# Two ABAB layers on one Trainium2 core: another layout of q and k in the attention, another order of its first steps

## The chip, the cores and the metric

The program runs on one core of one Trainium2 chip. The metric is the device time of one execution in microseconds (us); lower is better. A kernel is run several times and its median is given. Beside it there is one execution taken by the hardware profiler, whose rows are quoted here.

The engines are TensorE (PE in the profile, with its weight loads as PEld), VectorE (DVE), ScalarE (ACT), GpSimd (POOL) and SyncE (SP). PSUM is the small memory into which TensorE writes its sums, in banks of 512 float32 per partition; SBUF holds everything else, with 128 partitions.

## The reference

The program applies A, B, A, B to x (2048 tokens, 576 features), each with a layer norm ahead of it and a residual behind it; both A use the same weights, and so do both B. A is attention with 32 heads of 18 features. A token looks at itself and at the seven tokens at distances 2, 4, ..., 14 before it:

```
W, dil = (8, 2)
qkv = (x @ wqkv).reshape(B, S, 3, H, Dh)            # H = 32, Dh = 18
off = jnp.arange(W) * dil
idx = pos[:, None] - off[None, :]
mask = idx >= 0
...
logits = jnp.einsum('bhsd,bhswd->bhsw', q, kg) * Dh ** (-0.5)
logits = jnp.where(mask[None, None, :, :], logits, -1000000000.0)
o = jnp.einsum('bhsw,bhswd->bhsd', softmax(logits), vg) @ wo
```

B is a gated layer: gelu of x @ w_in (576 to 4608), a layer norm on its second half, a product over tokens with the 2048 x 2048 matrix w_sp, the product with the first half, and w_out back to 576 features.

## The kernel before

Activations are held in bfloat16, features on partitions (xnT) for matmuls that contract over features. The four layers follow each other in program order; there is no barrier between them, and each engine works through its own queue in order.

**The attention layer** (`layer_A`, once as the first layer, li = 0, once as the third, li = 2). Queries and keys of all heads stand in one SBUF tile QK of [128, 2, 8, 2048]: partitions, q or k, group, token. A head h lies in group g = h // 4, in the 32-partition slot j = h % 4: 18 partitions of data, then 14 "window rows", which hold a pattern that makes the logits of tokens outside the window so small that their exponential vanishes. The matmul over the 32 rows of a slot thus gives the masked logits of one head.

The window rows are written by VectorE (`fill_window_rows`, L198 and L201): four copies over all 128 partitions for each half of the tokens, each over one of q and k and four groups. They write over the data rows too, so the data come after them: half 0 of the data comes after `fill_window_rows(QK, 0)`, half 1 after `fill_window_rows(QK, 1)`.

The data come by way of a stage. A projection unit PG (L442; its matmuls are on L422) computes, for a chunk d of 128 features of q or of k (d = 0 to 3; d = 4 holds the last 64 features of q and of k) and a 512-token column cc, five matmuls into a PSUM bank; `evac` casts it into a stage tile (L403 on VectorE, L405 on ScalarE). When the four units of one chunk and one 1024-token half are there, one DMA per head and chunk ("move", issued through the helper on L78) carries the head's rows from the stage to its slot in QK, with two runs of 2 KB per partition (q and k). A head whose features straddle two chunks needs two moves. The moves go out alternately on two queues, GpSimd's and SyncE's; d = 4 needs a move each for q and k. SyncE also issues the transposes of the normalised input (L265).

Attention steps: the queries are cut into NT = 17 tiles (120 query columns each, 128 keys), each tile in two halves of 16 heads (groups 0 to 3, then 4 to 7), so NST = 34 steps s = 2t + half. Step loop: logits of the next step (`L_mm`, L496: 16 matmuls of 32 x 128), their exponential on ScalarE (`EXP`, L505), then the product with v of the present step (`PV`, L519, into a bank O_ps), which VectorE divides by the sums (reciprocal L525, product L527); then what a table has put at that step: the remaining projection units (cast by VectorE), the units VW that compute v, the output projection WO, loads, copies of the transposed output (`O_CP`).

PSUM in the steps: L_ps has four banks; all else (O_ps, pp, pv, pw) goes round through three banks, the ring "PT". A matmul into a bank waits until its last reader is done.

Before the steps: in the first attention the ten (chunk, column) pairs of half 0 are projected by PG units cast on ScalarE; then follow six units "pre" of the second half, whose casts k_ = 0 to 3 go to VectorE. After two of them comes `L_mm(0)`, after the fourth `fill_window_rows(QK, 1)`. In the third layer `PG_run` (L425) computes the units of d = 0, 1 and then 2, 3 with their banks all open, `on_dve` naming the units that VectorE casts; then `fill_window_rows(QK, 1)`, the two units of d = 4, four tiles of v, `L_mm(0)`, the six pre units and the steps.

In the first attention the layer norm of x runs just ahead, tile by tile: statistics S_ (L673), power on GpSimd (R_, L686: GpSimd does `R_(12, 4)` between moves), scaling A_ (L693), transpose T_ by DMA.

**Layer B** (L946, L1070, L1094, L1143) is dense matmuls. At its end each 128-token tile gets its residual, is stored, and is normalised for the next attention: statistics and power, with the scaling on ScalarE.

Of the kernel before, what the change touches and what calls it, by code (L numbers as in the profile page):

```python
# [18 lines left out]
P = 128  # L19
# [44 lines left out]
class K:  # L64
# [129 lines left out]
    def fill_window_rows(self, QK, half):  # L194
        nc, n = self.nc, self.cfg.S // 2
        for g0 in (0, 4):
            for a in range(2):
                nc.vector.tensor_copy(out=QK[:, a, g0:g0 + 4, half * n:(half + 1) * n].rearrange("p g (k x) -> p g k x", x=P),  # L198
                                      in_=self.pat[:, a, half, None, None, :].to_broadcast([P, 4, n // P, P]))
            if half == 0:  # L200
                nc.vector.tensor_copy(out=QK[:, :, g0:g0 + 4, 0:8], in_=self.pat0[:, :, None, :].to_broadcast([P, 2, 4, 8]))  # L201

# [137 lines left out]
    def layer_A(self, li):  # L340
# [11 lines left out]
        QK = main.tile([P, 2, 8, XW], bf16, name="QK")  # L352
        qT, kT = QK[:, 0], QK[:, 1]
        NSTG, CBW = (3 if li == 0 else 4), 1024
        stgs = [main.tile([P, 2, CBW], bf16, name=f"stg{k_}") for k_ in range(NSTG if li == 0 else 2)]
# [86 lines left out]
        def PG(d, qk, cc, dve, queues=(nc.sync, nc.gpsimd), pp=None):  # L442
# [18 lines left out]
            evac(stg[:, qk, gi * 512:(gi + 1) * 512], pp, dve)  # L461
            stg_left[key] -= 1
            if stg_left[key] == 0:
                stg_tiles.pop(key)
                cs = slice(cc * 512, (cc + 1) * 512) if alone else slice(cb * CBW, (cb + 1) * CBW)
                ss = slice(gi * 512, (gi + 1) * 512) if alone else slice(0, CBW)
                moves = []
                for h in range(d * P // DH, H):
# [14 lines left out]
        NST = 2 * NT  # L483
        L_tiles = {}
        owed = []

        def L_mm(s):
            t, hf = divmod(s, 2)
            nk, nq = tdim(t)
# [3 lines left out]
            for ftl in range(4):  # L493
                g = 4 * hf + ftl
                for j in range(4):
                    nc.tensor.matmul(L_tiles[s][j // 3][:nk, j % 3, ftl * P:ftl * P + nq],  # L496
                                     lhsT=kT[32 * j:32 * j + 32, g, k0_(t):k0_(t) + nk],
                                     rhs=qT[32 * j:32 * j + 32, g, q0_(t):q0_(t) + nq],
                                     start=True, stop=True, tile_position=(32 * j, 0))

        def EXP(s):
            nk, nq = tdim(s // 2)
            for jp, L_ps in enumerate(L_tiles.pop(s)):
                Lv = L_ps[:].rearrange("p a (b c) -> p a b c", c=P)
                nc.scalar.activation(out=P_bufs[2 * jp + s % 2][:nk, :, :, 0:nq], in_=Lv[:nk, :, :, 0:nq], func=ACT.Exp,  # L505
# [5 lines left out]
        def PV(s):  # L511
# [3 lines left out]
            for jp, js in enumerate(((0, 1, 2), (3,))):  # L515
                for ftl in range(4):
                    for jj, j in enumerate(js):
                        idx = 4 * ftl + j
                        nc.tensor.matmul(O_ps[:, idx * (DH + 1):(idx + 1) * (DH + 1)],  # L519
                                         lhsT=P_bufs[2 * jp + s % 2][:nk, jj, ftl, :],  # L520
# [24 lines left out]
        def O_CP(t):  # L545
# [710 lines left out]
```

## Time and profile before

| | us |
|---|---|
| median of 3 runs | 1163.04 (1162.76 to 1164.21) |
| profiled execution | 1164.2 |
| its span | 1162.4 |
| TensorE busy | 1146.0 |
| VectorE busy | 559.4 |
| ScalarE busy | 339.0 |
| GpSimd busy | 271.0 |

The profile's rows are read so. A row of a timeline has the start (us from the start of the span), the length, the engine, the line, the operation, the tiles written and read, the shape, the count of instructions that are drawn together, and in brackets the idle time before and what ended it. A row of waits has the engine and line that waited, what it waited for, the us in total, how often, and the longest. A row of windows has a stretch and the busy time of each engine in it, then the clock granted to TensorE (1.00 is full), the share of the DMA engines and GB/s. A row of the chain of waits has start, length, and who held the chain. "x11: 502/587/4973" is count and minimum, median and maximum in ns.

### The profile page before, as it was taken

How to read it: one execution, taken by the hardware profiler on the slowest of the kernel's cores; microseconds unless marked ns; L12 is line 12 of the kernel's file. 1: busy time of each engine (PE TensorE's matmuls, PEld its weight loads, DVE VectorE, ACT ScalarE, POOL GpSimd, SP SyncE). 2: the span in 40 equal slices, each digit the busy share in tenths (PEclk: the TensorE clock that was granted, in tenths of full speed). 3: DMA queues.
4: the chain of work that ended last, by engine and by line, in shares of the span. 5: the costliest groups of instructions: out<-in, count | busy, mean ns of one | idle time of the engine just before them, and what ended most of it. 6: DMA issues, size and time to landing. Idle time of an engine off the chain costs nothing.

```text
span 1162.4 us, 19969 instructions
## 1 busy us (share of the span) xinstructions
PE 1146.0 (99%) x8163; PEld 610.5 (53%) x8258; DVE 559.4 (48%) x1183; ACT 339.0 (29%) x503; POOL 271.0 (23%) x375
## 2 busy tenths in 40 slices
PE   9899999999999999999999999999999999999998
PEld 5467544444444444457755774444444444444677
DVE  8679888322233222235475888862322223322321
ACT  5499455011110111102247884541011110011000
POOL 3769855000000000001163776540000000000000
PEclk9899999999999999999999999999999999999999
DMA  9599796000000000049656997920000000001332
GB/s 214 114 177 291 199 219 132 23 12 12 12 2 11 12 12 1 19 138 297 172 102 117 229 245 183 259 55 4 8 12 12 12 12 1 12 1 47 114 104 74
DMA packets 184600, 106.59 MB, mean 92 GB/s; under 512 B 136201, under 2 KB 165545, under 8 KB 184509
## 3 DMA queue, kind: packets, MB, share of 16 engines
q1 hardware_dynamic: 171821, 86.04, 32.4%
q0 software_dynamic: 6096, 13.38, 4.4%
q10 hardware_dynamic: 6592, 5.90, 1.7%
q8 instruction: 64, 1.05, 0.4%
q14 instruction: 27, 0.22, 0.1%
HBM read 42.54 MB, written 21.77 MB: 55 GB/s over the span
## 4 chain that ended last, share of the span: by engine, by line
PE 94%; issue 1%; POOL 1%; ACT 1%; DVE 1%; DMA 1%; SPq 0%; ACTq 0%; DVEq 0%; POOLq 0%
PE pg L1094 43%; PE po L1143 12%; PE pz L946 6%; PE pz L1070 6%; PE pz1s L1070 6%; PE pzs L946 6%; PE pp L422 5%; PE pw L587 3%; PE O_ps L519 3%; PE pv L411 3%; PE L_ps L496 2%; POOL QK L78 1%; ACT P_sb L505 1%; DMA x_in<-in_A_x_dram 0%; DVE QK L198 0%
## 5 line engine op out<-in xcount | busy, mean ns | idle before, releaser
L1094 PE MATMUL pg<-Wq,Z 128*128 128x512 bf16 x2260 | 497.9, 379 | 2.5
L1094 PEld LDWEIGHTS <-Z 128*128 128x128 bf16 x2304 | 225.4, 98 | 271.8
L1098 DVE TENSOR_TENSOR g_tmp<-pg,ln_xn 128x512 f32<-128x512 f32 x144 | 99.6, 692 | 420.8 <-PE pg L1094 418.8
L1089 ACT ACTIVATE z1T<-pz 128x1024 bf16<-128x1024 f32 x36 | 34.9, 1021 | 500.8 <-PE pz L1070 500.8
L78 POOL DMA_DIRECT2D wout<-in_B_w_out_dram x4 | 4.3, 1073 | 598.8 <-PE pg L1094 598.8
L1143 PE MATMUL po<-wout,Z 128*128 128x288 bf16 x1152 | 141.4, 286 | 0.0
L505 ACT ACTIVATE P_sb<-L_ps 128x1440 bf16<-128x1440 f32 (+3 forms) x136 | 125.1, 972 | 23.0 <-PE L_ps L496 21.4
L1143 PEld LDWEIGHTS <-Z 128*128 128x128 bf16 x1152 | 112.7, 98 | 28.8
L946 PEld LDWEIGHTS <-xnT 128*128 128x128 bf16 (+1 forms) x800 | 68.2, 97 | 75.3 <-issue 9.7
L1099 DVE TENSOR_TENSOR Z<-g_tmp,z1T 128x512 bf16<-128x512 f32 x144 | 99.7, 692 | 13.0 <-DVE g_tmp L1098 0.9
L995 DVE BATCH_NORM_STATS2 z_st<-zp 128x6 f32<-128x512 bf16 (+1 forms) x160 | 91.5, 618 | 14.6 <-ACT zp L993 14.3
L1070 PEld LDWEIGHTS <-w 128*128 128x128 bf16 (+1 forms) x640 | 53.7, 97 | 74.0 <-issue 13.6
L422 PE MATMUL pp<-xnT,wqk_sb 128*128 128x512 bf16 (+1 forms) x313 | 76.4, 385 | 1.1 <-issue 0.2
L1153 DVE TENSOR_TENSOR x_new<-po,xo 128x288 f32<-128x288 f32 (+1 forms) x64 | 28.8, 455 | 88.4 <-PE po L1143 82.6
L1070 PE MATMUL pz<-xnT,w 128*128 128x512 bf16 (+1 forms) x316 | 66.3, 380 | 0.2
L1070 PE MATMUL pz1s<-xnT,w 128*128 128x512 bf16 (+1 forms) x310 | 64.9, 379 | 0.9 <-issue 0.8
L258 POOL TENSOR_SCALAR ln_xn<-x_new,ln_mv,ln_rstd 128x576 bf16<-128x576 f32 x28 | 64.1, 2289 | 2.6
L946 PE MATMUL pzs<-win2a,xnT 128*128 128x512 bf16 (+1 forms) x235 | 58.6, 358 | 0.4 <-issue 0.3
L946 PE MATMUL pz<-win2a,xnT 128*128 128x512 bf16 (+1 forms) x233 | 58.3, 357 | 0.4
L993 ACT ACTIVATE zp<-pz 128x1024 bf16<-128x1024 f32 (+2 forms) x56 | 36.6, 720 | 64.5 <-PE pz L946 64.5
L1019 POOL TENSOR_SCALAR Z<-zp,z_mv,z_rstd 128x256 bf16<-128x256 bf16 x32 | 54.4, 1701 | 3.8 <-POOL z_rstd L1011 0.4
L78 POOL DMA_DIRECT2D QK<-stg x76 | 46.9, 621 | 35.2 <-DVE stg L403 17.2
(124 smaller groups left out, 951.6 us busy)
## 6 DMA issues: line engine op xcount, KB each, us to landing
xres<-x_new SPq DMA_DIRECT2D x44, 288.0 KB
xo<-xres SPq DMA_DIRECT2D x32, 288.0 KB
wout<-in_B_w_out_dram POOLq DMA_DIRECT2D x4, 1296.0 KB, 7.9
xn_rows<-ln_xn SPq DMA_DIRECT2D x28, 160.0 KB
w<-in_B_w_in_dram SPq DMA_DIRECT2D x16, 256.0 KB
QK<-stg POOLq DMA_DIRECT2D x51, 72.0 KB, 4.7
xo<-xres SPq DMA_DIRECT2D x6, 576.0 KB
QK<-stg SPq DMA_DIRECT2D x37, 72.0 KB
```

The lines of the kernel that those rows point to most:

```text
L78: return eng.dma_start(out=out, in_=in_)
L258: e.tensor_scalar(out=xn[:nrows, 0:D], in0=x_t[:nrows, :], scalar1=mv[:nrows, 0:1], scalar2=rstd[:nrows, 0:1], op0=ALU.subtract, op1=ALU.mult)
L422: nc.tensor.matmul(pp, lhsT=w, rhs=self.xnT[r0:r1, c, cc * 512:(cc + 1) * 512], start=start, stop=stop, tile_position=(r0, 0))
L505: nc.scalar.activation(out=P_bufs[2 * jp + s % 2][:nk, :, :, 0:nq], in_=Lv[:nk, :, :, 0:nq], func=ACT.Exp, scale=scale)
L946: nc.tensor.matmul(out[:, o0:o0 + n], lhsT=self.xnT[r0:r1, c, r * P:(r + 1) * P], rhs=win2(c)[r0:r1, w0:w0 + n], start=start, stop=stop, t ...
L995: nc.vector.bn_stats(out=st[:, x // 512, :], in_=zp[:, x:x + min(512, w0 + n - x)])
L1019: eng.tensor_scalar(out=Z[:, b0:b1, i, :], in0=zv[:, b0:b1, :], scalar1=mv[:, 0:1], scalar2=rstd[:, 0:1], op0=ALU.subtract, op1=ALU.mult)
L1070: nc.tensor.matmul(outs[a_], lhsT=w1[r0:r1, c, sub * P:(sub + 1) * P], rhs=self.xnT[r0:r1, c, q * 512:(q + 1) * 512], start=start, stop=st ...
L1094: nc.tensor.matmul(pg[:, :], lhsT=Z[:, jj, i, sub * P:(sub + 1) * P], rhs=Wq[q][:, i, :], start=(i == 0), stop=(i == NS - 1))
L1098: nc.vector.tensor_tensor(out=tmp[:], in0=pg[:, :], in1=bsp[:, qs], op=ALU.add)
L1099: nc.vector.tensor_tensor(out=uT(jj)[:, sub, qs], in0=tmp[:], in1=z1Ts[jj, sub][:, qs], op=ALU.mult)
L1143: nc.tensor.matmul(acc[hh], lhsT=u_rows(j, i), rhs=wouts[j // NJH][:, j % NJH, hh * 288:(hh + 1) * 288], start=(j == 0), stop=(j == NJ - 1))
```

## The change

- QK becomes one flat tile of 16 x 2048 + 128 columns. Each group has 4 x 1024 columns: q of half 0, k of half 0, k of half 1, q of half 1. A stage holds q and k in that order too, so a move is one run of 4 KB per partition.
- d = 4 is cast as two copies of 64 partitions each (q and k side by side), and its heads are moved like the others. The first half then has 36 moves instead of 40.
- In the first attention the order of the steps is 0, 2, 4, 1, 3, 5, 6, ..., 16, 18, 17, 19, ...; P_bufs and the due times go by the position in this order.
- The tile of queries that crosses the halves (t = 8) takes 128 query columns, read in two pieces of 64.
- In the first attention `L_mm(0)` comes after three pre units instead of two.
- The moves of the first half: d = 0 to 2 alternate between SyncE and GpSimd (12 and 12), d = 3 and 4 all go on GpSimd (12).
- At the start, the load of one pattern row, one unit of v and some statistics stand in another place.
- In the third layer `PG_run` casts units 4 and 6 of d = 0, 1 on VectorE (before: 0, 1, 5, 7). The layer norm of the last tile at the end of layer B is scaled on VectorE, without the extra operand that ScalarE needed.
- `fill_window_rows` writes the same window rows, through the new layout.

```diff
     def fill_window_rows(self, QK, half):
         nc, n = self.nc, self.cfg.S // 2
+        QK = QK[:, 0:16 * self.cfg.S].rearrange("p (g b a n) -> p g b a n", g=8, b=2, a=2)
         for g0 in (0, 4):
             for a in range(2):
-                nc.vector.tensor_copy(out=QK[:, a, g0:g0 + 4, half * n:(half + 1) * n].rearrange("p g (k x) -> p g k x", x=P),
+                nc.vector.tensor_copy(out=QK[:, g0:g0 + 4, half, a ^ half, :].rearrange("p g (k x) -> p g k x", x=P),
                                       in_=self.pat[:, a, half, None, None, :].to_broadcast([P, 4, n // P, P]))
...
-        QK = main.tile([P, 2, 8, XW], bf16, name="QK")
-        qT, kT = QK[:, 0], QK[:, 1]
         NSTG, CBW = (3 if li == 0 else 4), 1024
+        CROSS = 2 * CBW + P // 2
+        QK = main.tile([P, 16 * XW + P], bf16, name="QK")
...
-            evac(stg[:, qk, gi * 512:(gi + 1) * 512], pp, dve)
+            gs = slice(gi * 512, (gi + 1) * 512)
+            if d < 4:
+                evac(stg[:, qk ^ cb, gs], pp, dve)
+            else:
+                for a_ in range(2):
+                    evac(stg[0:64, a_ ^ cb, gs], pp[64 * a_:64 * a_ + 64, :], dve)
...
-                    if d < 4:
-                        moves.append((QK[q0:q0 + n, :, g, cs], stg[s0:s0 + n, :, :]))
+                    dst, src = QK[q0:q0 + n, (2 * g + cb) * 2 * CBW:(2 * g + cb + 1) * 2 * CBW], stg[s0:s0 + n, :, :]
+                    if alone:
+                        moves.append((dst.rearrange("p (a c) -> p a c", a=2)[:, :, ss], src[:, :, ss]))
                     else:
-                        for a_ in range(2):
-                            moves.append((QK[q0:q0 + n, a_, g, cs], stg[64 * a_ + s0:64 * a_ + s0 + n, 0, ss]))
+                        moves.append((dst, src.rearrange("p a c -> p (a c)")))
...
+        seq = list(range(NST))
+        if li == 0:
+            seq[0:6] = [0, 2, 4, 1, 3, 5]
+            seq[17:19] = [18, 17]
+        pos = {s: p_ for p_, s in enumerate(seq)}
...
+        def qspan(t):
+            q0, nq = q0_(t), tdim(t)[1]
+            return (k0_(t), P) if q0 < CBW < q0 + nq else (q0, nq)
...
+        def span(j, g, a, x0, n):
+            cb, x = divmod(x0, CBW)
+            g0 = 4 * g * CBW
+            o0 = g0 + (2 * cb + (a ^ cb)) * CBW + x
+            rows = QK[32 * j:32 * j + 32]
+            if x + n <= CBW or a == 1:
+                return rows[:, o0:o0 + n]
+            return rows[:, g0:g0 + 2 * CROSS].rearrange("p (b c) -> p b c", c=CROSS)[:, :, x:CBW]
...
-                                     lhsT=kT[32 * j:32 * j + 32, g, k0_(t):k0_(t) + nk],
-                                     rhs=qT[32 * j:32 * j + 32, g, q0_(t):q0_(t) + nq],
+                                     lhsT=span(j, g, 1, k0_(t), nk), rhs=span(j, g, 0, q0, nq),
...
-            B_(4)
+            rows[2](nc.sync)
             A_(3)
-            G_(4)
+            VW(2, 0, False)
             T_pe(3)
...
-            S_(5)
+            S_(4, 5)
             R_(4, 2)
-            rows[2](nc.sync)
...
-                    PG(d, qk, cc, False, (nc.gpsimd, nc.sync) if d in (0, 4) else q2)
+                    PG(d, qk, cc, False, (nc.gpsimd, nc.sync) if d < 3 else (nc.gpsimd,))
...
-                       (0, 1, 5, 7) if d0 == 0 else (1, 3, 5, 7),
+                       (4, 6) if d0 == 0 else (1, 3, 5, 7),
...
-            if k_ == (2 if li == 0 else 0):
+            if k_ == (3 if li == 0 else 0):
                 self.ring = ["PT"]
                 L_mm(0)
                 EXP(0)
...
-                L_mm(s + 1)
-                EXP(s + 1)
-            PV(s)
+                L_mm(seq[s + 1])
+                EXP(seq[s + 1])
+            PV(seq[s])
...
-                mv, rstd, nmr = self.ln_stats(p3, x_new, P)
-                xns[i] = self.ln_xn(x_new, P, mv, rstd, nmr, eng="act")
+                on_dve = i == NS - 1
+                mv, rstd, nmr = self.ln_stats(p3, x_new, P, want_nmr=not on_dve)
+                xns[i] = self.ln_xn(x_new, P, mv, rstd, nmr, eng="dve" if on_dve else "act")
```

More of the change, by code (lines that the diff above doesn't have):

```diff
@@ L464, in PG @@
                 stg_tiles.pop(key)
-                cs = slice(cc * 512, (cc + 1) * 512) if alone else slice(cb * CBW, (cb + 1) * CBW)
-                ss = slice(gi * 512, (gi + 1) * 512) if alone else slice(0, CBW)
+                ss = slice(gi * 512, (gi + 1) * 512)
                 moves = []
@@ L545, in O_CP @@
         def O_CP(t):
+            d0 = q0_(t) - qspan(t)[0]
             for c0, a, n in ring_parts(t):
-                nc.vector.tensor_copy(out=oT[:, :, c0:c0 + n], in_=o_slots[(t // 2) % NSLOT][:, :, a:a + n])
+                nc.vector.tensor_copy(out=oT[:, :, c0:c0 + n], in_=o_slots[(t // 2) % NSLOT][:, :, d0 + a:d0 + a + n])
         def O_T(t):
@@ L716, in layer_A @@
                     VW(t, hh, False)
-            B_(4)
+            rows[2](nc.sync)
             A_(3)
-            G_(4)
+            VW(2, 0, False)
             T_pe(3)
-            for t in (2, 3):
-                for hh in range(2):
-                    VW(t, hh, False)
+            VW(2, 1, False)
+            VW(3, 0, False)
+            VW(3, 1, False)
             x3 = sb.tile([P, 4, D], bf16, name="x_in3", tag="x_in", bufs=2)
```

22 lines of the change are left out of this document (12 added, 10 removed).

## The prediction

> **What bounds the kernel now.** I read the page first, then who waited for whom on TensorE, then the timeline and the granted clock of the stretch that this named.
>
> ```profile
> PE 1146.0 (99%) x8163; PEld 610.5 (53%) x8258; DVE 559.4 (48%) x1183; ACT 339.0 (29%) x503; POOL 271.0 (23%) x375
> ...
> PE L_ps L496 <- DMA QK<-win2a: 3.5, 4, 2.8
> ```
>
> TensorE (PE) is busy 1146.0 of 1162.4 us, so a change that leaves its matmuls alone can only win idle time, or time at a low clock. About a fifth of the 16.4 us between is one wait: the second logits step of the first attention waits 3.5 us for the moves of the last heads into QK.
>
> ```profile
> 46.63 0.35 PE L496 MATMUL L_ps<-QK 32*128 32x128 bf16 x12
> 47.22 0.21 PE L496 MATMUL L_ps<-QK 32*128 32x128 bf16 x1 [0.25 <-DMA QK<-win2a]
> 50.22 0.28 PE L496 MATMUL L_ps<-QK 32*128 32x128 bf16 x1 [2.78 <-DMA QK<-win2a]
> ...
> 58.97 0.39 PE L496 MATMUL L_ps<-QK 32*128 32x120 bf16 x16
> ...
> 60.89 0.39 PE L496 MATMUL L_ps<-QK 32*128 32x120 bf16 x16
> ```
>
> One undisturbed step takes 60.89 - 58.97 = 1.92 us. Four steps lie between 46.63 and 60.89, so without a disturbance the last of them would start at 46.63 + 4 x 1.92 = 54.31. The hole costs 60.89 - 54.31 = 6.6 us: 3.5 us of waiting, and 3.1 us that the next rows explain (busy times per engine, then the granted clock PEclk).
>
> ```profile
> 48.00:50.00 2.00, 0.00 (x0) 0.00 (x0) 0.78 (x1) 0.00 (x0) 1.87 (x3) 0.98 0.45 103
> 50.00:52.00 2.00, 1.35 (x20) 0.86 (x21) 0.00 (x0) 0.96 (x1) 0.00 (x0) 0.50 0.09 23
> ...
> 56.00:58.00 2.00, 2.00 (x37) 0.92 (x36) 0.72 (x3) 1.07 (x3) 2.00 (x5) 0.81 0.34 52
> ```
>
> After the pause the clock is 0.50 until about 56.8. Why the moves were late stands in the chain of waits, in the moves of GpSimd (POOL; minimum, median and longest issue in ns) and in VectorE's (DVE) rows:
>
> ```profile
> 42.20 2.63 POOL QK L78 x4
> 44.83 4.03 issue
> 48.87 0.50 POOL QK L78
> 49.37 1.80 DMA QK<-win2a
> ...
> 59.04 0.33 PE L_ps L496 x16
> 59.37 0.50 PE O_ps L519 x16
> 59.86 1.09 PE pp L422 x5
> ...
> L78 POOL DMA_DIRECT2D QK<-win2a x11: 502/587/4973, 40.3 to 55.7; - x11
> ...
> 44.15 4.62 DVE L198 COPY QK<-win_pat 128x4096 bf16<-128x4096 bf16 x4
> 52.07 0.26 DVE L525 RECIPROCAL rec<-O_ps 128x16 f32<-128x16 f32 x1 [3.29 <-PE O_ps L519]
> 52.36 0.46 DVE L527 TENSOR_TENSOR o_t<-O_ps,rec 128x288 bf16<-128x288 f32 x1
> ```
>
> One move took 4.973 us to issue where the median is 0.587. It ends at 48.87, just after VectorE's four copies that fill the window rows of the second half (44.15 to 48.77). The last two moves come behind it and land 1.80 us after their issue.
>
> **The change, part by part.** *Step order.* The steps become 0, 2, 4, 1, ..., so heads 16 to 31 (groups 4 to 7) are first read by the fourth logits step instead of the second: two steps, 3.8 us, later. By itself that takes the whole wait of 3.5 us away.
>
> *The fill gets a wait that it did not have.* QK is now one flat tile in which a group holds q and k of the first half, then k and q of the second. A window-row copy writes one quarter of each of four groups, and in the order and waits of the built program it counts as touching all that lies between. So the copies for the second half wait: those of groups 0 to 3 for the moves of heads that lie in groups 1 to 3, those of groups 4 to 7 for the moves in groups 5 to 7. In the kernel before, the same copies wait for no move. VectorE works in order, so what is queued behind them waits too: in the first attention the reciprocal and product that empty the first O_ps bank, in the second attention the casts of the six projection units ahead of the steps. TensorE needs those PSUM banks (three of them).
>
> First attention, from these rows of GpSimd and of the transfers (count, size, median to landing):
>
> ```profile
> 29.65 9.64 POOL L78 DMA_DIRECT2D QK<-stg  x15 [5.43 <-ACT stg L405]
> 39.32 1.04 POOL L686 TENSOR_TENSOR lnx_rstd<-lnx_rstd,neg_half 128x4 f32<-128x4 f32 x1
> ...
> L78 POOL DMA_DIRECT2D QK<-stg x15: 520/577/1632, 29.7 to 38.7; - x15
> ...
> QK<-win2a POOLq DMA_DIRECT2D x3, 36.0 KB, 1.8
> ```
>
> GpSimd keeps 24 moves, 12 ahead of its power L686 and 12 behind it. Twelve take 1.63 + 11 x (9.64 - 1.63)/14 = 7.9 us, to 37.6; the power lasts to 38.6. A move with single runs took 0.502 at the least, one with two runs 0.587 in the median; I take 0.54, which puts ten of the last twelve before the fill (43.9, as the casts ahead of it no longer wait for the power, at most 0.4 earlier than before). The eleventh is caught by the fill's first two copies (2.3 us, to 46.2), two more moves take it to 47.2, and the last lands 1.8 later, at 48.7 (47.0 if none is caught; 50.0 if three are left and land after some 2.2). Then the second two copies (2.3), reciprocal and product (52.07 to 52.82, 0.75) free the bank at 51.75. TensorE is there at 46.63 + 1.92 + 0.33 + 0.50 = 49.4. It waits 2.35 us, and 0.2 more one step later, where VectorE is still catching up. Of 6.6 us, 2.55 are still lost: a gain of 4.05 at full clock (2.7 to 5.5 with the bounds above). Half of the old hole would be mended; and a pause of 2.35 us is not far below the one that halved the clock.
>
> *Second attention.* Rows of before (TensorE, VectorE, GpSimd, transfers):
>
> ```profile
> 596.39 2.53 PE L422 MATMUL L_ps<-xnT,wqk_sb 128*128 128x512 bf16 x11 [0.40 <-ACT stg L405]
> ...
> 611.53 0.40 PE L496 MATMUL L_ps<-QK 32*128 32x128 bf16 x16
> 611.86 6.65 PE L422 MATMUL pp<-xnT,wqk_sb 128*128 128x512 bf16 x29
> 618.44 0.40 PE L496 MATMUL L_ps<-QK 32*128 32x128 bf16 x16
> ...
> 605.18 4.66 DVE L198 COPY QK<-win_pat 128x4096 bf16<-128x4096 bf16 x4
> 613.15 0.69 DVE L403 CAST stg<-pp 128x512 bf16<-128x512 f32 x1 [3.32 <-PE pp L422]
> ...
> 603.07 10.20 POOL L78 DMA_DIRECT2D QK<-stg  x14 [0.58 <-ACT stg L405]
> ...
> QK<-stg POOLq DMA_DIRECT2D x15, 72.0 KB, 5.1
> QK<-stg POOLq DMA_DIRECT2D x4, 36.0 KB, 2.9
> ```
>
> The last layer norm goes to VectorE and fewer of the first casts do, so the wait of 0.40 us on ScalarE's late cast goes: -0.4. But the fill, which ran at 605.18 beside the moves, now runs behind them. Its first half waits for two moves issued from 602.7 on, 5.1 us to landing without the fill's own delay: about 607.5 to 609.8. GpSimd's last move of chunk 3 is issued by about 609.8 (eleven moves from 602.7 at 0.54 to 0.73, the mean of 10.20/14 under the fill) and lands 2.9 to 5.1 us later; I take 613.7 (612.6 to 615.3). The second half of the fill ends at 616.0, the first cast behind it at 616.7. TensorE starts logits at 611.1, has 0.33 + 3 x 1.09 us of work until its three banks are full at 614.7, and waits 2.0 us (0.9 to 3.6). Three more units put the second logits at 616.7 + 3.3 = 620.0. The three moves of chunk 4 are now issued behind the fill: 616.0 + 3 x 0.54 + 1.8 to 2.9 = 619.4 to 620.5, which adds 0.2 (0 to 0.5). So 620.2 instead of 618.44: a loss of 1.75 us net of the 0.4 (0.5 to 3.7).
>
> *The rest.* Chunk 4 is cast as two copies of 64 partitions instead of one (0.69 on VectorE, in steps where it is busy some 1.4 of 1.92 us): 0 to +0.4, taken +0.1, since three banks cover one late cast. The pattern loads and statistics at the start move a little: -0.4 to 0, taken -0.1. The tile that crosses the halves has 128 columns instead of 120, and two casts more per chunk on ScalarE: inside its slack. The 4 KB runs themselves save at most 0.587 - 0.502 = 0.085 us of a queue per move, already in the 0.54. The Trainium skill ("DMA: Bandwidth & Descriptors", why small descriptors are slow) says that transfers within SBUF do not suffer from small descriptors; by that the landing gains nothing from longer runs, and by these rows the sum holds no such gain either way.
>
> The longest pause of TensorE at full clock that left the clock alone:
>
> ```profile
> 7.34 0.79 PE L411 MATMUL pv<-wv_sb,xnT 128*128 128x288 bf16 x5 [0.79 <-ACT xnT L702]
> ```
>
> **Sum**, against the profiled execution (1164.2 us, span 1162.4, some 1.2 above the median of the runs; the differences are put on the median 1163.04): -4.05 + 1.75 + 0.1 - 0.1 = -2.3 at full clock, and +3.1 for each of the two pauses that halves the clock. That pause was 0.79 us; the one with a drop was 2.78 plus 0.25. Pauses of 2.35 and 2.0 lie between, nearer to the second. I give the first one even odds and the second four in ten, so exactly one drop is likeliest: 1163.04 - 2.3 + 3.1 = 1163.8.
>
> **The rivals.**
> *No drop.* Both pauses stay too short or straddle what the gate watches: 1163.04 - 2.3 = 1160.7. For it: both estimates are below 2.78. The Trainium skill ("TensorE: Matmul & The Clock Gate", on oscillation) names idle gaps over some 3.4 us as what re-throttles; here one of 3.0 us with one matmul in it did, so the rule as stated is too kind, and the table of windows decides.
> *Slower: VectorE held in the second attention, at half clock.* Both pauses drop the clock: 1163.04 - 2.3 + 6.2 = 1166.9. The deciding place is the second attention, where nothing was lost before: with the last landing of chunk 3 after 613.7 the pause is over 2.0 us, and with a drop this stage loses 1.75 + 3.1 = 4.85, more than the first attention wins. For it: the banks are full at 614.7 whatever the moves do; against it: a pause of 2.0 is shorter than the known one.
> *The fill's waits are met in time* (the moves land before VectorE is needed, or the copies wait for less than I read): then the first attention wins the whole 6.6, the second its 0.4: 1163.04 - 7.0 = 1156.0. Against it: the last moves of before are issued up to 49.9, and those of chunk 3 land after 611.
>
> **How the numbers follow.** One drop 0.42 (1163.8, own range 1161.3 to 1166.3), no drop 0.25, two drops 0.23, waits met 0.10. A difference of 0.2% (2.3 us) is about what a measurement of this kernel can tell from no change. Faster by more is all of "waits met", half of "no drop" and little of "one drop": 0.10 + 0.12 + 0.03 = 0.25. Slower by more: 0.8 of "two drops" and a fifth of "one drop": 0.18 + 0.09 = 0.27. Between: 0.48. The range that leaves out 2 in 10 runs from 1159.0 (no drop with the bounds of the first pause; most of "waits met" is left out) to 1167.4.
>
> **What would show it.** Right: no wait of the logits line for QK in the first attention; VectorE idle between the two halves of the second-half fill, released by a transfer into QK, near 46 to 48.7 and 610 to 613.7; TensorE waiting on VectorE near 49.4 and 614.7; no wait at 596.4. The clock beside these two pauses says which case it was. Wrong: fill copies back to back, or moves landing before 46 and 610; or a new wait in a later step, where groups are read in the other order.

## The result, and the profile after

| | before | after |
|---|---|---|
| median, runs side by side | 1163.62 us (1159.72 to 1166.14, 6 runs) | 1174.25 us (1170.22 to 1179.45, 6 runs) |
| profiled execution | 1164.2 | 1174.14 |
| its span | 1162.4 | 1172.4 |

The ratio is 1.0095 (95% interval 1.0072 to 1.0118): slower. Forecast were 1163.8 us in a range of 1159.0 to 1167.4.

Which wait costs most stands in the view of TensorE's waits after the change (line of the matmul, releaser, total us, count, longest):

```profile
PE pp L424 <- DVE o_t L551: 5.4, 2, 4.6
PE pp L424 <- DVE stg L405: 2.3, 1, 2.3
PE L_ps L521 <- issue: 1.7, 1, 1.7
```

The 3.5 us for QK<-win2a are gone and VectorE is the releaser instead. I set the starts of the logits steps of the two traces against each other. The lead or lag of after (plus is late) is +0.1 us at the second step, -5.4 at the third, -0.7 at the fourth and +0.2 at the fifth, so the whole gain of the new order is lost again within two steps. Then it grows to +3.3 by 118 us, +4.2 by the end of the first layer B (587.9 before), falls to +3.6 at the casts of the next attention, jumps to +7.7 across that attention's second logits, to +9.6 at 640, and ends at +10.0. Now each place.

**First attention.** Timeline of VectorE after (start, duration, then what ended the idle time before):

```profile
44.09 2.35 DVE L199 COPY QK<-win_pat 128x4096 bf16<-128x4096 bf16 x2
51.06 2.36 DVE L199 COPY QK<-win_pat 128x4096 bf16<-128x4096 bf16 x2 [4.62 <-DMA QK<-win2a]
...
53.62 0.46 DVE L551 TENSOR_TENSOR o_t<-O_ps,rec 128x288 bf16<-128x288 f32 x1
```

and of TensorE:

```profile
48.99 0.56 PE L543 MATMUL O_ps<-v_ext,P_sb 128*128 128x19 bf16 x16
54.14 2.31 PE L424 MATMUL pp<-xnT,wqk_sb 128*128 128x512 bf16 x5 [4.58 <-DVE o_t L551]
```

The second pair of fill copies waits 4.62 us for a move into QK; reciprocal and product stand behind it on VectorE, and TensorE gets no bank until 54.14. The clock is low until 58.6 (0.85 in the last of these windows is 0.6 us at half) (windows; the column ahead of the DMA share is the granted clock):

```profile
50.00:52.00 2.00, 0.00 (x0) 0.00 (x0) 0.94 (x1) 0.99 (x2) 0.00 (x0) 0.94 0.00 0
52.00:54.00 2.00, 0.00 (x0) 0.00 (x0) 1.97 (x5) 0.00 (x0) 0.00 (x0) 0.50 0.00 0
...
58.00:60.00 2.00, 1.82 (x36) 0.99 (x36) 1.01 (x2) 1.41 (x3) 0.00 (x0) 0.85 0.64 195
```

Why did the move land so late, when GpSimd was early? These are the issue of GpSimd's last first-half move and the issues of SyncE's transposes, after the change:

```profile
44.36 1.05 POOL L78 DMA_DIRECT2D QK<-win2a  x1 [0.18 <-issue]
```

```profile
38.81 6.63 SPq L266 DMA_TRANSPOSE xnT<-ln_xn  x4
```

and the transposes before, which start 3.7 us later:

```profile
42.49 5.38 SPq L265 DMA_TRANSPOSE xnT<-ln_xn  x4
```

The last move is issued at 44.36, and its issue takes 1.05 us beside the fill where the others take 0.50. But it lands 6.5 us later, at 50.9. Before, the last one was issued at 49.37 and landed at 51.16, so an issue that is 5.0 us earlier brought a landing that is 0.3 us earlier. The transfers of 36 to 52 us, after (queue with its packets, MB and share of the 16 engines; moves by size with the median to landing):

```profile
q1 hardware_dynamic: 2887, 1.17, 61.8%
...
QK<-win2a POOLq DMA_DIRECT2D x9, 72.0 KB, 6.5
```

and before:

```profile
q1 hardware_dynamic: 3029, 1.16, 42.7%
...
QK<-win2a POOLq DMA_DIRECT2D x4, 72.0 KB, 3.9
```

SyncE's queue moves as much as before (1.17 to 1.16 MB) but keeps the engines busy for 61.8 instead of 42.7%, and GpSimd's moves land in 6.5 instead of 3.9 us. These two executions alone do not show that the change is the reason. e4 and e12 below leave the instructions of the first attention as they are before (e12 adds one memset and moves later tiles), and there the same four moves land in 7.1 and 6.7 us, with SyncE's queue at 51.4 and 55.8%. The rows of e4:

```profile
q1 hardware_dynamic: 3062, 1.22, 51.4%
...
QK<-win2a POOLq DMA_DIRECT2D x4, 72.0 KB, 7.1
```

What all the profiled executions say together stands behind e16.

**Between 70 and 90 us** VectorE waits for transposes of o_t, which it does not do before (rows of after):

```profile
71.86 0.46 DVE L551 TENSOR_TENSOR o_t<-O_ps,rec 128x288 bf16<-128x288 f32 x1 [1.97 <-DMA oT<-o_t]
...
87.79 0.35 DVE L572 COPY oT<-o_slot 128x600 bf16<-128x600 bf16 x1 [1.16 <-DMA o_slot<-o_t]
```

TensorE loses 0.87 us behind the first, 0.72 behind the second.

**Layer B** starts with a wait on zp, after:

```profile
137.03 0.81 PE L970 MATMUL pz<-win2a,xnT 128*128 128x512 bf16 x3 [0.70 <-ACT zp L1017]
```

```profile
135.95 1.94 ACT L1017 ACTIVATE zp<-pz 128x1024 bf16<-128x1024 f32 x2 [2.02 <-POOL ln_xn L259]
```

ScalarE's first write of zp now waits for ln_xn on GpSimd; before, the same write (at 129.30) waits for TensorE's pz. QK is now 256 bytes longer per partition, so later tiles lie elsewhere, and zp may share memory with a tile of that layer norm; e12 tests this.

**Second attention**, after, TensorE and VectorE, and the clock:

```profile
600.00 2.54 PE L424 MATMUL L_ps<-xnT,wqk_sb 128*128 128x512 bf16 x11
...
621.17 5.08 PE L424 MATMUL pp<-xnT,wqk_sb 128*128 128x512 bf16 x15 [2.28 <-DVE stg L405]
```

```profile
612.11 2.36 DVE L199 COPY QK<-win_pat 128x4096 bf16<-128x4096 bf16 x2 [3.23 <-DMA QK<-stg]
618.15 2.36 DVE L199 COPY QK<-win_pat 128x4096 bf16<-128x4096 bf16 x2 [3.68 <-DMA QK<-stg]
```

```profile
620.00:622.00 2.00, 0.83 (x4) 0.44 (x4) 2.00 (x4) 0.00 (x0) 0.95 (x2) 0.95 0.04 12
622.00:624.00 2.00, 2.00 (x7) 0.66 (x5) 1.00 (x2) 0.00 (x0) 0.55 (x2) 0.50 0.40 119
624.00:626.00 2.00, 2.00 (x8) 0.69 (x6) 0.69 (x1) 0.00 (x0) 0.00 (x0) 0.70 0.00 0
```

The row at 600.00 has no wait any more: the 0.40 us on ScalarE's cast are gone. Both halves of the fill wait, TensorE pauses 2.28 us, and the clock is low for some 3.4 us after it: (0.05 + 0.50 + 0.30) x 2 = 1.7 us lost. One more place follows, a logits step that stops in its midst:

```profile
646.53 0.28 PE L521 MATMUL L_ps<-QK 32*128 32x120 bf16 x5 [1.73 <-issue]
```

The row names no releaser, but a move of GpSimd's that was issued at 636.45 lands at 646.53, 10.1 us later, just when TensorE goes on.

### The profile page after: what moved, and what is told of

Its sections match the earlier page's. It is cut to its first block, busy times and chain, and to the rows that moved or that the text cites. A ratio compares the mean times of both kernels' runs of the same rounds, so it can differ in the third digit from the quotient of the medians.

```text
span 1172.4 us, 19946 instructions
## 1 busy us (share of the span) xinstructions
PE 1148.3 (98%) x8163; PEld 611.5 (52%) x8258; DVE 560.9 (48%) x1187; ACT 341.7 (29%) x507; POOL 253.3 (22%) x364
## 3 DMA queue, kind: packets, MB, share of 16 engines
q8 instruction: 64, 1.05, 0.4%
## 5 line engine op out<-in xcount | busy, mean ns | idle before, releaser
L529 ACT ACTIVATE P_sb<-L_ps 128x480 bf16<-128x480 f32 (+3 forms) x136 | 125.5, 976 | 33.1 <-PE L_ps L521 31.1
L970 PE MATMUL pzs<-win2a,xnT 128*128 128x512 bf16 (+1 forms) x235 | 58.6, 358 | 0.4 <-issue 0.3
L424 PEld LDWEIGHTS <-wqk_sb 128*128 128x128 bf16 (+1 forms) x360 | 32.8, 99 | 46.1 <-issue 8.1
```

The lines of the kernel that those rows point to most:

```text
L424: nc.tensor.matmul(pp, lhsT=w, rhs=self.xnT[r0:r1, c, cc * 512:(cc + 1) * 512], start=start, stop=stop, tile_position=(r0, 0))
L529: nc.scalar.activation(out=P_bufs[2 * jp + pos[s] % 2][:nk, :, :, 0:nq], in_=Lv[:nk, :, :, 0:nq], func=ACT.Exp, scale=scale)
L970: nc.tensor.matmul(out[:, o0:o0 + n], lhsT=self.xnT[r0:r1, c, r * P:(r + 1) * P], rhs=win2(c)[r0:r1, w0:w0 + n], start=start, stop=stop, t ...
```

## The experiments

Ratios are to the kernel before, run beside on the same chip, with the 95% interval. Where two ratios of experiments are compared, the difference is uncertain by some 3.4 to 4.6 us to either side (the root of the sum of the squares of both intervals). Four theories run through them: T1, the fill's wait holds VectorE; T2, moves and transposes are late because they share queues and engines; T3, the new order bunches the transposes of o_t; T4, runs of 4 KB delay the landing.

**e1, the fill group by group.**

```diff
+        step = 4 if half == 0 else 1
-        for g0 in (0, 4):
+        for g0 in range(0, 8, step):
```

> The changed kernel with the window rows of the second half filled group by group (16 copies of 1024 columns instead of 4 of 4096), so that no fill copy waits for a move any more. Theory 1 (the fill's wait holds VectorE and so TensorE): the pauses of 4.58 and 2.28 us go with both drops of the clock, some 6 and 4 us, and what was added in later steps (some 6 us) stays: 1164 us. Rival, theory 2 (the moves land late whatever the fill does, because the transposes of tiles 12 to 15 now run beside them): the fourth logits step then waits for QK near 50 us, the first hole stays and only the second attention wins: 1168 to 1170.

1167.92 us (4 runs), ratio 1.0063 (1.0041 to 1.0086). VectorE and TensorE in e1:

```profile
43.48 5.45 DVE L200 COPY QK<-win_pat 128x1024 bf16<-128x1024 bf16 x16
48.83 0.26 DVE L550 RECIPROCAL rec<-O_ps 128x16 f32<-128x16 f32 x1
```

```profile
51.76 1.24 PE L425 MATMUL pp<-xnT,wqk_sb 128*128 128x512 bf16 x5 [2.81 <-DMA xnT<-ln_xn]
...
618.67 0.40 PE L522 MATMUL L_ps<-QK 32*128 32x128 bf16 x16
```

Sixteen copies run without a break, the bank is free at 49.6, and the pause of the second attention is gone. So T1's mechanism holds: both pauses that VectorE ended are gone. By the ratios the false waits cost 3.7 us, as much as the uncertainty of the difference (by the medians, from two chips, 1174.25 - 1167.92 = 6.3). But the time is not the 1164 of theory 1, it is just below the range of theory 2, and the kernel stays slower than before: TensorE now waits 2.81 us for a transpose of xnT, not for QK, the clock falls behind this wait (52.9 to 56.3 us), and at 588 it is 0.8 us late again.

**e2, e1 with the old step order.**

```diff
-            seq[0:6] = [0, 2, 4, 1, 3, 5]
-            seq[17:19] = [18, 17]
```

> As e1, with the steps of the first attention in their old order. Theory 3 (the new order brings three transposes of the attention output close together and VectorE waits for them at 70 to 88): those waits, 2.7 us, go; but the second step needs all moves again, which landed at 50.9, so TensorE waits some 4 us near 47 and its clock drops: 1163 to 1167, the hole of 6 to 7 us back. If order is not the cause, the waits at 70 to 88 stay and the time is above 1169.

1170.29 (4 runs), 1.0086 (1.0066 to 1.0106), above the 1163 to 1167 that theory 3 gave. The old hole is back:

```profile
PE L_ps L521 <- DMA QK<-win2a: 3.4, 3, 2.5
```

Of VectorE's waits for transposes of o_t at 70 to 88 us one of 0.72 us is left. But e1, with the new order, has only 0.16 and 0.42 us of them, so these two runs do not make the order their cause.

**e3, before with the new step order alone.**

```diff
+            seq[0:6] = [0, 2, 4, 1, 3, 5]
+            seq[17:19] = [18, 17]
```

> The kernel before with the new step order alone. Theory 1 (order is good in itself, the flat layout spoils it): the hole of 6.6 us goes: 1156.5 to 1158. Theory 3 (the order itself costs waits for transposes later): 1159 to 1161, with VectorE waiting for o_t at 65 to 90.

1160.17 (10 runs), 0.9987 (0.9971 to 1.0003): the time is in theory 3's range, but its sign is missing: no wait of VectorE for o_t appears, so the order alone is not what makes transposes late (T3 falls). TensorE's pauses, and the clock, in e3:

```profile
48.74 1.25 PE L422 MATMUL pp<-xnT,wqk_sb 128*128 128x512 bf16 x5 [0.36 <-DVE o_t L532]
...
50.96 0.58 PE L501 MATMUL L_ps<-QK 32*128 32x128 bf16 x3 [0.64 <-DMA QK<-win2a]
52.38 0.58 PE L524 MATMUL O_ps<-v_ext,P_sb 128*128 128x19 bf16 x16 [0.84 <-DVE win2a L403]
```

```profile
52.00:54.00 2.00, 1.32 (x18) 0.89 (x19) 1.93 (x6) 1.39 (x2) 1.38 (x3) 0.59 0.08 18
```

Behind three pauses of 0.36, 0.64 and 0.84 us the clock is halved, though none of them is long. The second one is a wait for QK: with the order alone, 0.64 us of the old wait stay.

**e4, before with the last layer norm on VectorE and (4, 6) as its casts.**

```diff
-                       (0, 1, 5, 7) if d0 == 0 else (1, 3, 5, 7),
+                       (4, 6) if d0 == 0 else (1, 3, 5, 7),
+                on_dve = i == NS - 1
```

> The kernel before with the last layer norm on VectorE and units 4 and 6 cast there. As predicted: the wait of 0.40 us goes, 1162.6 to 1163.4. Rival: VectorE's fill of the first half starts later, the moves follow it, and the second logits step of the second attention waits: 1163.6 or more.

1162.05 (10 runs), 0.9999 (0.9977 to 1.0022). The wait of 0.40 us is gone and the trace is 0.56 us ahead there; in the time it is too little to be seen.

**e5 and e7, runs of 2 KB in e1 and in the change.** The stages are 16 columns wider, so a move's q and k no longer touch.

```diff
-        stgs = [main.tile([P, 2, CBW], bf16, ...
+        stgs = [main.tile([P, 2, CBW + 16], bf16, ...
-                        moves.append((dst, src.rearrange("p a c -> p (a c)")))
+                        moves.append((dst.rearrange("p (a c) -> p a c", a=2), src[:, :, 0:CBW]))
```

> As e1 (fill group by group), with 16 spare columns between q and k in the stages, so that each move has two runs of 2 KB per partition again instead of one of 4 KB; same layout of QK, same order, same queues. Theory 4 (runs of 4 KB on SyncE's queue keep each DMA engine longer per descriptor, so the transposes and the last moves land late): the transposes of tiles 12 to 15 land before 48 and the pause of 2.8 us on xnT goes, 1160 to 1163. Theory 2 (they land late because they are issued 4 us earlier and so run beside the moves): nothing changes, 1166 to 1169.

> The changed kernel itself with runs of 2 KB again (spare columns in the stages), the fill as in the change. Theory 4: the last first-half move lands near 48.7 as predicted instead of 50.9 and the waits for transposes at 70 to 90 go: 1166 to 1169. Theories 1 and 2: 1173 to 1175, no change.

e5: 1166.43 (5 runs), 1.0043 (1.0013 to 1.0074). e7: 1169.30 (4 runs), 1.0067 (1.0045 to 1.0088). Both carry a side effect of the edit: the wider stages shift memory once more, and the wait for zp is

```profile
PE pz L971 <- ACT zp L1018: 3.3, 1, 3.3
```

instead of 0.7, 2.6 us more in their traces (row of e5; e7 has the same, and there the clock falls behind it too, from 138.4 to 141.8 us). In spite of it e7 is 3.3 us faster than the change by the ratios, within the uncertainty. Transfers of 36 to 52 us in e5, and in e1 with 4 KB:

```profile
q1 hardware_dynamic: 3009, 1.17, 52.2%
...
QK<-win2a POOLq DMA_DIRECT2D x9, 72.0 KB, 5.1
```

```profile
q1 hardware_dynamic: 2866, 1.11, 61.8%
...
QK<-win2a POOLq DMA_DIRECT2D x9, 72.0 KB, 6.9
```

The same nine moves land in 5.1 us with 2 KB runs and in 6.9 with 4 KB, and e5 has no wait for xnT any more, as theory 4 had it; its time lies in theory 2's range. e7's time is just above theory 4's 1166 to 1169, and its trace speaks against theory 4 in the first attention: its nine moves land in 6.3 us where the change has 6.5, the last one at 50.77 us and not near 48.7, and TensorE's pause is 5.09 us. Its gain lies elsewhere: in the second attention the pause is 0.41 instead of 2.28 us, and of the waits at 70 to 90 us one of 1.86 is left. One pair of executions does not settle T4.

**e6 and e8, the old sharing of queues in e1 and in e5.**

```diff
-                    PG(d, qk, cc, False, (nc.gpsimd, nc.sync) if d < 3 else (nc.gpsimd,))
+                    PG(d, qk, cc, False, (nc.gpsimd, nc.sync) if d in (0, 4) else q2)
```

> As e1, with the old sharing of the moves of the first half (d = 1 to 3 alternating, starting as before, d = 4 alternating), so that SyncE has about 16 moves and the transposes come after them. Theory 2: the moves are done sooner, the wait for QK or xnT near 50 shrinks below 1.5 us, 1162 to 1165. Theory 4: the transposes land as late or later, 1167 or more.

> Fill by group, old sharing of the moves and runs of 2 KB: of the change only the flat layout without its waits, the step order, the third pre unit, the start and the tail are left. If these parts are good as predicted, it is at least as fast as the kernel before with the new order alone: 1157 to 1160. If layout or start cost something by themselves: above 1162.

e6: 1168.16 (10 runs), 1.0049 (1.0020 to 1.0078); e8: 1169.36 (9 runs), 1.0072 (1.0045 to 1.0099). Neither differs from its partner by more than the intervals, and here 2 KB is no better even with the 2.6 us taken off. So no cost of the new sharing is seen, and e8, above 1162, says that layout or start cost something by themselves.

**e9 to e12.** e9 takes all of the change but the layout; e10 and e11 take two parts each; e12 only shifts memory.

```diff
+        qk_pad = main.tile([P, P], bf16, name="qk_pad")
+        nc.gpsimd.memset(qk_pad[:, 0:1], 0.0)
```

(the diff of e12; e9 to e11 consist of the parts as they stand in the change)

> The kernel before plus every part of the change except the layout of QK: step order, start of the kernel, third early unit, sharing of the moves among the queues, last layer norm on VectorE. QK keeps q and k apart in runs of 2 KB, the fill waits for no move, and zp keeps its old memory. If the layout and what hangs on it (the fill's waits, 4 KB runs, the other memory of zp) is the whole cause, the first hole is all but gone, nothing is given back between 70 and 90 us, and the time is 1157 to 1160, as with the step order alone or a little below. If the sharing of the queues and the start make moves and transposes late whatever the layout, there are new DMA waits at 70 to 90 us, as in the kernel with a fill by group, and the time is 1164 to 1168.

> The kernel before plus the step order and the new sharing of the moves of the first attention (chunks 0 to 2 alternate between GpSimd and SyncE, 3 and 4 on GpSimd alone); nothing else. With the step order alone the ratio was 0.9987. If the sharing of queues makes transposes and moves late, waits of 1 us and more for o_slot, oT or QK appear at 70 to 90 us and the ratio rises to 1.002 or more; if it does not, the time stays within 1 us of the step order alone, some 1160 to 1161.

> The kernel before plus two parts of the change that paid in runs of their own: the step order (1.0 to 2.8 us) and the last layer norm of the first layer on VectorE (0.1 to 0.6 us). If they add, 1158.5 to 1161.0 and a ratio of 0.996 to 0.999; if the gain of the order is one of chance in when the clock drops, the ratio is 1.000 with a drop of the clock in the first attention as before.

> The kernel before with an unused tile of 256 bytes per partition behind QK (one element of it is set by GpSimd), so that all later tiles lie 256 bytes further, as in the change; nothing else. If the wait of TensorE for zp at 137 us in the change comes from the memory that zp then shares with another tile, it shows here as well, 0.7 to 3.3 us at 133 to 138 us, and the time is 0.5 to 3 us above the kernel before. If the wait comes from the step order or from late moves, nothing shows there and the time is that of the kernel before.

e9: 1165.22 (11 runs), 1.0020 (1.0001 to 1.0039): the range given for queues and start as a cause. But its profiled execution, the fastest of the eleven, keeps the gain of the first attention to the end (-2.6 us at 588) and has one wait of 0.9 us between 75 and 90, so what the other ten lost isn't seen. e10: 1160.62 (11 runs), 0.9993 (0.9969 to 1.0017): queues cost nothing to be seen. e11: 1162.17 (12 runs), 0.9982 (0.9958 to 1.0006), its ratio as expected and its median above. e12: 1163.36 (11 runs), 1.0010 (0.9987 to 1.0033), and its trace has the wait:

```profile
132.18 0.81 PE L948 MATMUL pz<-win2a,xnT 128*128 128x512 bf16 x3 [0.70 <-ACT zp L995]
```

256 bytes of unused memory bring the 0.70 us, with zp's first write waiting for ln_xn as in the change; that cause is shown, the effect on the time is too small for the interval.

In e10 the hole is mended: the logits that waited before (the fourth step of the new order, at 51.20) and the clock beside them have nothing left of it:

```profile
51.20 0.40 PE L501 MATMUL L_ps<-QK 32*128 32x128 bf16 x16
```

```profile
50.00:52.00 2.00, 2.00 (x42) 1.12 (x39) 1.91 (x4) 1.75 (x3) 1.05 (x3) 1.00 0.03 8
```

**e13 to e15, the start and the third unit.** e13 adds the changed start to e10, e14 the third early unit; e15 takes both away from e1.

```diff
-            if k_ == (2 if li == 0 else 0):
+            if k_ == (3 if li == 0 else 0):
```

(e14; e13 and e15 move the lines of the start as in the change, forth and back)

> The kernel before plus step order, new sharing of the queues and the changed start (window rows 2 loaded earlier, the V units between the statistics, statistics 4 and 5 together); the layout of QK stays. Order and queues alone gave 1160.62 with the clock at 1.0 in 10 of 11 runs, all parts but the layout 1165.22 with a lower clock in 6 of 11. If the start is what costs, by leaving waits at 50 to 53 us that halve the clock in some runs, this gives 1163 to 1166 and a lower clock in about half of the runs; if it is the third early unit, 1160 to 1161.5.

> The kernel before plus step order, new sharing of the queues and the third projection unit ahead of the first logits; layout and start as before. If the third unit is what costs (VectorE and ScalarE have one more cast between the last early move and the first step), 1163 to 1166 and a lower clock in about half of the runs; if it is the start, 1160 to 1161.5 with waits below 0.6 us at 48 to 53 us.

> The change with the fill of the second half group by group (no wait for moves), and start and early units as before: so the layout with 4 KB runs, step order, queues and last layer norm. With the new start and third unit it took 1167.92. If those two cost as much with this layout as with the old one (about 4.6 us), 1162.5 to 1164.5; if the layout alone makes the transposes late by its 4 KB runs (the wait for xnT of 2.8 us at 51 us stays), 1166 to 1169.

e13: 1164.63, 1.0013 (0.9992 to 1.0035). e14: 1164.27, 1.0011 (0.9992 to 1.0030). e15: 1167.43, 1.0049 (1.0024 to 1.0074); 11 runs each. Each of the two parts seems to cost some 2 us, but the intervals overlap with e10's, and a clock below 0.999 came in 3 and 4 of 11 runs where half were expected; it is not settled. e15 decides the other question: with the old start the layout still costs, 1.0049 against 0.9993.

**e16 and e17, the two ends of that comparison on one chip**: e15 with 2 KB runs (the edit of e5), and before with order, queues and last layer norm.

> The kernel with the layout, the fill by group and the old start (1167.43), with staging tiles 16 columns wider, so that a move is two runs of 2 KB per partition again instead of one of 4 KB. The wider tiles shift memory further: the wait for zp at 138 us is expected at 3.3 instead of 0.7 us, 2.6 us more. If the 4 KB runs make the transposes and moves late, the waits for xnT at 52 us and for o_t at 73 to 89 us shrink and the time is 1162 to 1165 in spite of zp (less than 1163 without it). If the layout costs by something else, the waits stay and the time is 1168 to 1171.

> The kernel before plus the three parts of the change that cost nothing where they were run: step order, new sharing of the queues, last layer norm on VectorE. If they add, 1158.5 to 1161 and a clock of 0.999 or more in nearly all runs, ratio 0.996 to 0.999; if the gain of the order in e3, e10 and e11 was chance, the ratio lies at 1.000 with a lower clock in a third of the runs, as in the kernel before.

e16: 1166.41 (11 runs), 1.0037 (1.0015 to 1.0058), with zp's 2.6 us in it. e17: 1161.08 (11 runs), 0.9992 (0.9973 to 1.0012). Transfers of 36 to 52 us in e15 and e16:

```profile
q1 hardware_dynamic: 2904, 1.20, 76.9%
...
QK<-win2a POOLq DMA_DIRECT2D x9, 72.0 KB, 7.7
```

```profile
q1 hardware_dynamic: 2964, 1.09, 55.0%
...
QK<-win2a POOLq DMA_DIRECT2D x9, 72.0 KB, 5.2
```

Here 7.7 us to landing stand against 5.2; TensorE's wait for the transposed xnT goes from 1.9 to 1.0 us, and e16's time lies between the expectations of the two theories. All nineteen profiled executions together decide about the transfers. The median landing of GpSimd's moves into QK that are issued from 36 to 52 us is 6.2 to 7.9 us in the five with runs of 4 KB (the change, e1, e2, e6, e15) and 3.8 to 6.5 in the fourteen with 2 KB; the share of SyncE's queue in this stretch is 61.1 to 76.9% against 40.8 to 59.5%. So longer runs do go with later landings and a busier queue (T4 holds for the transfers), by less than single executions differ. What this costs in time is not shown: by the ratios 2 KB saves 1.4 (e15, e16), 2.3 (e1, e5), 3.3 (the change, e7) and -2.7 us (e6, e8), with the 2.6 us for zp 4.0, 4.9, 5.9 and -0.1. The layout costs 6.5 us here (1.0049 - 0.9993 of 1162), more than the uncertainty of 4.0.

No version beats both kernels for certain: e3 (0.9987) and e11 (0.9982) come nearest, and their intervals hold 1.

## Why the prediction was wrong, point by point

The ratios make a chain from before to after: the order -0.0013 (e3), the queues +0.0006 (e10), start, third unit and last layer norm +0.0027 (e9), the layout with a fill that waits for nothing +0.0043 (e1), the fill's waits +0.0032. In us (times 1162): -1.5 + 0.7 + 3.1 + 5.0 + 3.7 = 11.0. The first link has an interval of 1.9 us to both sides, the others of some 3.5; the link of the layout is larger than its interval, that of the fill just as large, the other three can't be told from 0.

- *The new order by itself takes the whole wait of 3.5 us away.* Right in e10; in e3, with the order alone, 0.64 us of it stay. But the hole of 6.6 us was that of one execution. By the same reckoning (second to sixth logits step, less 4 x 1.92) it is 4.4 us in e4 and 3.1 in e12, whose first attention has the same instructions: they wait 2.1 and 2.3 us for QK instead of 3.5, none of their moves takes more than 1.6 us to issue where the prediction saw 4.97, and the clock is low for 3.4 us in e4 and never in e12. Of 121 runs of before taken in these comparisons, 68 have a mean granted clock of 0.999 or more and a median of 1161.0, and 40 have less than 0.998 and a median of 1166.3. So the order is worth less against the median than against that execution: 1.5 us by e3, with an interval that holds 0.
- *The fill's false waits.* Right in mechanism and places: VectorE idle between the halves, released by a transfer into QK, TensorE released by VectorE, in both attentions (e1 takes both pauses away).
- *"The last lands 1.8 later, at 48.7."* This is the term that failed in the first attention. The issue was sooner than I worked out (44.36, held up by the fill for 0.5 us instead of 2.3), but the landing took 6.5 us, not 1.8: 50.9, a pause of 4.58 us instead of 2.35, outside the bounds of 47.0 to 50.0. The 1.8 us came from the last moves of before in one execution, where they were issued when all four transposes were out. In e4 and e12 such moves are issued beside the transposes and land in 4.9 and 4.2 us, with the same instructions. So an earlier issue does not bring the landing forward by as much; in the change the moves run beside all four transposes and in runs of 4 KB, and how the 6.5 us divide between the two is not shown. The expected gain of 4.05 us came out as a loss of 0.2: 2.2 went with the longer pause and about as much with the half clock, which I had given even odds (full pace again at 58.6, 4.5 us after TensorE went on). The upper bound of that gain, with a last landing at 47.0, comes to 5.7 by the prediction's own steps, not 5.5; nothing hangs on it.
- *The 4 KB runs save at most 0.085 us of a queue per move, and the landing gains nothing.* The issue is shorter as foreseen (0.50), but the landing is rather longer: 6.9 against 5.1 (e1, e5), 7.7 against 5.2 (e15, e16) and 6.5 against 6.3 us (the change, e7). I had bounded this term from the side of a gain alone. The Trainium skill ("DMA: Bandwidth & Descriptors", why small descriptors are slow) says that transfers within SBUF do not suffer from small descriptors; the traces agree in that moves in runs of 2 KB land no later than in runs of 4 KB in these three pairs.
- *Second attention.* Pause 2.28 us where 2.0 (0.9 to 3.6) was forecast, VectorE as releaser, the wait of 0.40 us gone: right. The clock fell, for which I gave four in ten, but for 3.4 us, a loss of 1.7 rather than 3.1. TensorE lost 3.6 us up to the second logits, where 1.75 and 3.1 make 4.85.
- *Nothing was foreseen for 70 to 118 us (3.1 us), for zp (0.9 by the trace) and for 640 to 650 us (1.9).* At the first and the last place moves of the second halves and transposes of o_t land late; I had costed the first halves alone. They run beside each other before, too, so why they are later here stays open. The second comes from 256 bytes of memory, which the diff shows as a wider tile and nothing else.
- *Rivals.* That both pauses drop the clock (1166.9) is what happened, in places and order. It is 7.3 us below the measured median. In the traces the kernels lie 10.0 us apart where this rival had 3.9. Of the 6.1 us between, the first attention makes 1.2 (the pause longer by 2.2, the half clock cheaper by 0.9), the three unforeseen places 5.9, the second attention -1.3, and small differences the rest.

Open: why the layout costs more than its 4 KB runs, the false waits and zp together; and whether the start and the third unit cost anything, as e13 and e14 hint; and what of the landing time comes from the runs of 4 KB and what from the transposes. Five of the profiled executions (e6, e8, e13, e15, e16) hold one wait of 3.4 to 4.7 us that ends between 81 and 91 us:

```profile
83.80 0.48 PE L501 MATMUL L_ps<-QK 32*128 32x120 bf16 x16 [4.25 <-issue]
```

(e13, where the five moves that GpSimd issues from 72.15 to 74.82 us land 11 to 13 us after their issue). What keeps moves for so long was not found.

## What to carry to other kernels

A landing time from one trace holds for that execution and for the traffic it was measured in: before a schedule lets moves run beside transposes, take the landing from rows that had both, and from several executions. A wait that ends in a landing need not get shorter when the issue comes sooner. A tile that is made flat so that transfers get longer runs also changes what a strided writer is taken to touch, and whose memory the later tiles share; list the waits of the built program for every writer of the tile and for tiles far behind it. When a kernel's runs have a spread from the clock, compare a gain with the median run and not with the execution that the profiler happened to take.

## What the runs showed of the hardware that was not expected

The clock does not need one long pause: 2.28 us were enough in the second attention of the change, pauses of 0.36, 0.64 and 0.84 us within 4.0 us in e3, and 0.56, 0.51 and 0.47 us within 2.0 us in e14 (ending at 43.58):

```profile
44.00:46.00 2.00, 2.00 (x7) 0.77 (x6) 0.32 (x1) 1.85 (x2) 2.00 (x5) 0.57 0.80 115
```

Nor does the sum alone decide. In e12 pauses of 1.53, 0.38 and 0.38 us within 2.8 us are followed by a full clock, and so are three pauses of 1.76 us in sum within 3.6 us in e9:

```profile
50.05 1.24 PE L422 MATMUL pp<-xnT,wqk_sb 128*128 128x512 bf16 x5 [0.89 <-DMA xnT<-ln_xn]
...
51.85 0.22 PE L501 MATMUL L_ps<-QK 32*128 32x128 bf16 x1 [0.17 <-DMA QK<-win2a]
52.77 0.55 PE L524 MATMUL O_ps<-v_ext,P_sb 128*128 128x19 bf16 x16 [0.70 <-DVE win2a L403]
```

```profile
54.00:56.00 2.00, 2.00 (x39) 1.03 (x37) 1.71 (x5) 0.89 (x1) 2.00 (x5) 1.00 0.37 62
```

So between some 1.5 and 2.3 us of idling in a few us it is open whether the clock falls, and executions of the same instructions differ by it: in the first attention it is low for 6.8 us in before, for 3.4 in e4 and not at all in e12. Each low stretch that ends within a trace's span lasts 3.4 us or twice that. The Trainium skill ("TensorE: Matmul & The Clock Gate", on oscillation) names gaps over some 3.4 us; here less was enough, and the measurement decides.

The landing of a move differs from execution to execution of the same instructions: the four moves of 72 KB from 36 to 52 us land in 3.9 us in before, 7.1 in e4 and 6.7 in e12, and the share of SyncE's queue is 42.7, 51.4 and 55.8% for 1.16 to 1.30 MB. Which resource moves and transposes share was not measured.
